# Decode attention over 65,536 keys on one core: every key chunk in the repeated code, alternating order of scores and values, second buffers

## The chip, the cores and the metric

The kernel runs on one core of one Trainium2 chip. The metric is the device time of one execution in microseconds. The profiler recorded one execution on the same core; "us" below is microseconds, and moments are counted from the first instruction of that execution.

## The reference

One query token, 32 query heads, 8 key/value heads, so that four query heads share one key/value head. Keys and values are bf16, 65,536 x 128 for each of the 8 heads: 134 MB of keys and 134 MB of values.

```python
B, Hq, Hkv, Sq, Sk, D = 1, 32, 8, 1, 65536, 128
k = jnp.repeat(k, rep, axis=1); v = jnp.repeat(v, rep, axis=1)
scores = jnp.einsum("bhqd,bhkd->bhqk", q, k) * D ** -0.5
p = _softmax(scores, axis=-1)
return jnp.einsum("bhqk,bhkd->bhqd", p, v)
```

## The kernel before

**Chunks.** Each head's keys are cut into four chunks of 16,384 keys, so there are 32 chunks (`NU`), and the key and value loads of chunk n are called K0 to K31 and V0 to V31 here. One load is 4,194,304 bytes: 128 partitions with 128 tiles of 128 values each. There are two buffers for keys (`kbuf`) and two for values (`vbuf`), so chunk n uses buffer n % 2.

**Loads.** SyncE issues every load on one DMA queue in the order K0, K1, V0, K2, V1, K3, V2, and so on. Before K(n) it waits for `kfree`, which ScalarE raises when TensorE has finished the transposes of chunk n-2. Before V(n) it waits for `vfree`, which VectorE raises when the value sum of chunk n-2 is done. A waiting load holds back all loads behind it in that order. K0 and K31 come in two pieces with semaphores of their own (`kpiece`), V31 in four (64, 32, 16 and 16 tiles, `vpiece`). The queries are loaded ahead of K0 on the same queue.

**TensorE.** A key tile must be transposed before it can be multiplied with the queries. The transposes go in 16 groups of eight tiles (`pe_transposes`). Each group lands in one of four PSUM buffers (`trb`) and is copied to `ktb` in SBUF (`evict`): three of four groups by VectorE, every fourth by ScalarE. The scores of a group (`pe_scores`) follow three groups later (`LAG`), so the transposes of group 15 are followed by the scores of group 12, and three score groups are still to come. `pe_values` multiplies the 128 value tiles of a chunk with its probabilities. `pe_pass(u)` runs the keys of chunk u+1 together with the values of chunk u: all transposes, with scores following; then the values of chunk u; then the last three score groups of chunk u+1. `passes` writes out the pass u = -1 (keys of chunk 0 alone), then a loop of 15 turns with two passes each, then the passes 30 and 31. Pass 31 has only the values of chunk 31.

**VectorE and the softmax.** For chunk u, `dve_pass(u)` first takes the value sum of chunk u-1 (L195), raises `vfree` (L196) and adds it to `acc`. Then it takes the finished scores of chunk u (`qkd`, L207) and reduces them to one maximum a partition (L212). It copies the first three groups of chunk u+1 and then waits for GpSimd's maximum over the partitions (L297, back through `cma`). It sets the new running maximum and hands the negated one to ScalarE (`ng`, L225 or L229). It copies the middle groups of chunk u+1, rescales the sums, and copies the last groups. ScalarE computes the probabilities into `pts` (L276), with four exponentials a chunk, and then tells TensorE that the values may start (`exd`).

**Start and end.** GpSimd builds the identity matrix (L292, L293) and VectorE casts it (L256). TensorE transposes the queries with it, and VectorE lays them out for the first head. Then TensorE waits for the first piece of K0. At the end VectorE adds the last value sum and divides by the sum of the probabilities (L202). TensorE transposes the result (L169), VectorE casts it (L263), and SyncE writes it out (L337).

Of the kernel before, what the change touches and what calls it, by code (L numbers as in the profile page):

```python
# [5 lines left out]
DT = mybir.dt  # L6
AF = mybir.ActivationFunctionType
ALU = mybir.AluOpType
# [7 lines left out]
NKG = 8  # L16
LAG = 3
HU = 4
K_PIECES = (64, 64)
V_PIECES = (64, 32, 16, 16)  # L20


# [10 lines left out]
def bass_standalone__gqa_softmax__decode_kernel(nc, q, k, v, out):  # L33
# [15 lines left out]
    def sem(name):  # L49
# [2 lines left out]
    kbuf = [sb(f"kbuf{i}", [P, T * D], DT.bfloat16) for i in range(2)]  # L52
    vbuf = [sb(f"vbuf{i}", [P, T * D], DT.bfloat16) for i in range(2)]
    ktb = sb("ktb", [P, NKG * TB * P], DT.bfloat16)
    pts = sb("pts", [P, T * R], DT.bfloat16)
    qsb = sb("qsb", [HR, D], DT.bfloat16)
    qT = sb("qT", [P, HR], DT.bfloat16)
    qtmp = sb("qtmp", [P, HR], DT.bfloat16)
# [18 lines left out]

    trb = [S(nc.psum_tensor(f"trb{i}", [P, TB * P], DT.bfloat16)) for i in range(NTB)]
    qkb = [S(nc.psum_tensor(f"qkb{i}", [P, T * R], DT.float32)) for i in range(2)]
    pvb = S(nc.psum_tensor("pvb", [P, 512], DT.float32))  # L80

    krdy = [sem(f"krdy{i}") for i in range(2)]
    vrdy = [sem(f"vrdy{i}") for i in range(2)]
    kpiece = [sem(f"kpiece{i}") for i in range(len(K_PIECES))]
    vpiece = [sem(f"vpiece{i}") for i in range(len(V_PIECES))]
    kfree = [sem(f"kfree{i}") for i in range(2)]
    vfree = [sem(f"vfree{i}") for i in range(2)]
# [3 lines left out]
    xd, xa, xg = sem("xd"), sem("xa"), sem("xg")  # L91
    q_sem, o_sem, s_x, t_if, t_id, t_qT, t_o, t_row = (
        sem(n) for n in ("q_sem", "o_sem", "s_x", "t_if", "t_id", "t_qT", "t_o", "t_row"))


    def has_k(u):
        return u + 1 < NU
# [13 lines left out]
    def pe_transposes(pe, n, j):  # L111
        b = n % 2
        kv = kbuf[b][:, :].rearrange("p (t d) -> p t d", d=D)
        pieced = n in (0, NU - 1)
        for i in range(TB):
            t = j * TB + i
            if not pieced and t == 0:
                take(pe, krdy[b], 16)
            if pieced and t in (0, K_PIECES[0]):
                take(pe, kpiece[t > 0], 16)  # L120
            ins = pe.transpose(trb[j % NTB][:, i * P:(i + 1) * P], kv[:, t, :], ident[:, :])  # L121
        ins.then_inc(tra if on_act(j) else trd, 1)

# [8 lines left out]
        if j == G - 1:  # L132
            ins.then_inc(qkd, 1)

    def pe_values(pe, u):
        vv = vbuf[u % 2][:, :].rearrange("p (t d) -> p t d", d=D)
        starts = [sum(V_PIECES[:i]) for i in range(len(V_PIECES))]
        for t in range(T):
            if u < NU - 1 and t == 0:
                take(pe, vrdy[u % 2], 16)  # L140
            if u == NU - 1 and t in starts:
                take(pe, vpiece[starts.index(t)], 16)
            if t == 0:
                take(pe, exd)
            ins = pe.matmul(pvb[:, 0:R], lhsT=vv[:, t, :], rhs=pts[:, t * R:(t + 1) * R],  # L145
                            start=t == 0, stop=t == T - 1)
        ins.then_inc(pvd, 1)

    def pe_pass(pe, u):
        pend = []  # L150
        if has_k(u):
            for j in range(G):
                pe_transposes(pe, u + 1, j)
                pend.append(j)
                if len(pend) > LAG:
                    pe_scores(pe, u + 1, pend.pop(0))
        if u >= 0:
            pe_values(pe, u)
        while pend:
            pe_scores(pe, u + 1, pend.pop(0))  # L160

    def tensor_engine(pe):
        pe.wait_ge(q_sem, 16)
        pe.wait_ge(t_id, 1)
        pe.transpose(trb[0][:, 0:HR], qsb[:, :], ident[0:HR, 0:HR]).then_inc(s_x, 1)  # L165
        pe.wait_ge(t_qT, 1)
        passes(pe, lambda u: pe_pass(pe, u), 0, 2, NU - 1)
        pe.wait_ge(t_o, 1)
        pe.transpose(qkb[0][0:HR, 0:P], oT[:, :], identf[:, :]).then_inc(s_x, 1)  # L169

# [16 lines left out]
    def next_queries(e, inc):  # L187
        e.tensor_copy(qcur[:, :], qT[:, 0:R]).then_inc(inc, 1)
        own(e, e.tensor_copy(qtmp[:, 0:HR - R], qT[:, R:HR]), xd)
        own(e, e.tensor_copy(qT[:, 0:HR - R], qtmp[:, 0:HR - R]), xd)  # L190

    def dve_pass(e, u):
        w = u - 1
        if w >= 0:
            take(e, pvd)  # L195
            e.sem_inc(vfree[w % 2], 1)  # L196
            if w % HU == 0:
                own(e, e.tensor_copy(acc[:, :], pvb[:, 0:R]), xd)  # L198
            else:
                own(e, e.tensor_tensor(acc[:, :], acc[:, :], pvb[:, 0:R], ALU.add), xd)  # L200
            if w % HU == HU - 1:
                e.tensor_tensor(oT[:, HR - R:HR], acc[:, :], recip[:, :], ALU.mult).then_inc(  # L202
                    t_o if w == NU - 1 else xd, 1)
                if w < NU - 1:
                    take(e, xd)
        if 0 <= u < NU:
            take(e, qkd)  # L207
            if u % HU == HU - 1 and has_k(u):
                next_queries(e, qrdy)
            elif has_k(u):  # L210
                e.sem_inc(qrdy, 1)
            e.tensor_reduce(cmax[:, :], qkb[u % 2][:, :].rearrange("p (t g) -> p g t", g=R),  # L212
                            AX.X, ALU.max).then_inc(cm, 1)
        if u >= NU:
            return
        part = [[j for j in range(a, b) if not on_act(j)] for a, b in ((0, 4), (4, 12), (12, G))]
        if has_k(u):
            for j in part[0]:
                evict(e, u + 1, j)
        if u >= 0:  # L220
            take(e, cma)
            mn, mo = m[u % 2], m[(u - 1) % 2]
            if u % HU == 0:
                e.tensor_copy(mn[:, :], cmaxa[:, :])  # L224
                e.tensor_scalar(negm[:, :], cmaxa[:, :], -scale, None, ALU.mult).then_inc(ng, 1)  # L225
            else:
                own(e, e.tensor_tensor(mn[:, :], mo[:, :], cmaxa[:, :], ALU.max), xd)
                e.tensor_tensor(dm[:, :], mo[:, :], mn[:, :], ALU.subtract)  # L228
                e.tensor_scalar(negm[:, :], mn[:, :], -scale, None, ALU.mult).then_inc(ng, 1)  # L229
        if has_k(u):  # L230
            for j in part[1]:
                evict(e, u + 1, j)
        if u >= 0:
            take(e, sx)
            if u % HU == 0:
                own(e, e.tensor_copy(lp[:, :], rsum[:, :]), xd)
            else:
                own(e, e.tensor_tensor(acc[:, :], acc[:, :], alpha[:, :], ALU.mult), xd)
                own(e, e.tensor_tensor(lp[:, :], lp[:, :], alpha[:, :], ALU.mult), xd)  # L239
                own(e, e.tensor_tensor(lp[:, :], lp[:, :], rsum[:, :], ALU.add), xd)  # L240
            if u % HU == HU - 1:
                e.sem_inc(lrd, 1)
        if has_k(u):
            for j in part[2]:
                evict(e, u + 1, j)
        if u % HU == HU - 1 and u >= 0:
            take(e, lra)
            own(e, e.reciprocal(recip[:, :], la[:, :]), xd)
            own(e, e.tensor_copy(otmp[:, 0:HR - R], oT[:, R:HR]), xd)
            own(e, e.tensor_copy(oT[:, 0:HR - R], otmp[:, 0:HR - R]), xd)  # L250

    def vector_engine(e):
        e.memset(oT[:, :], 0.0).then_inc(xd, 1)
        take(e, xd)
        e.wait_ge(t_if, 1)
        e.tensor_copy(ident[:, :], identf[:, :]).then_inc(t_id, 1)  # L256
        e.wait_ge(s_x, 1)
        own(e, e.tensor_copy(qT[:, :], trb[0][:, 0:HR]), xd)
        next_queries(e, t_qT)
        e.sem_inc(qrdy, 1)  # L260
        passes(e, lambda u: dve_pass(e, u), 1, HU, NU)
        e.wait_ge(s_x, 2)
        e.tensor_copy(orow[:, :], qkb[0][0:HR, 0:P]).then_inc(t_row, 1)  # L263


    def act_pass(e, u):
        if has_k(u):
            evict(e, u + 1, 3)
        if u >= 0:
            take(e, ng)  # L270
            if u % HU:
                e.activation(alpha[:, :], dm[:, :], AF.Exp, scale=scale)  # L272
            sv = qkb[u % 2][:, :].rearrange("p (t g) -> p g t", g=R)
            pv = pts[:, :].rearrange("p (t g) -> p g t", g=R)
            for g in range(R):
                ins = e.activation(pv[:, g, :], sv[:, g, :], AF.Exp, bias=negm[:, g:g + 1],  # L276
                                   scale=scale, accum_out=rsum[:, g:g + 1])
            own(e, ins, xa)
            e.sem_inc(exd, 1)
            e.sem_inc(sx, 1)  # L280
        if has_k(u):
            for j in (7, 11, 15):
                evict(e, u + 1, j)

    def scalar_engine(e):
        e.wait_ge(t_if, 1)
        e.activation(dscr[:, 0:1], identf[:, 0:1], AF.Exp, scale=1.0)
        passes(e, lambda u: act_pass(e, u), 1, HU, NU - 1)
# [14 lines left out]
    def sync_engine(e):  # L303
# [10 lines left out]
        def load_k(n):  # L314
            if n >= 2:
                e.wait_ge(kfree[n % 2], n // 2)
            if n in (0, NU - 1):
                pieces(kbuf[n % 2], src(kf, n), K_PIECES, kpiece)
            else:
                e.dma_start(kbuf[n % 2][:, :], src(kf, n)).then_inc(krdy[n % 2], 16)  # L320

        def load_v(n):
            if n >= 2:
                e.wait_ge(vfree[n % 2], n // 2)
            if n == NU - 1:
                pieces(vbuf[n % 2], src(vf, n), V_PIECES, vpiece)
            else:
                e.dma_start(vbuf[n % 2][:, :], src(vf, n)).then_inc(vrdy[n % 2], 16)

        e.dma_start(qsb[:, :], qf).then_inc(q_sem, 16)  # L330
        load_k(0)
        for u in range(NU):
            if has_k(u):
# [40 lines left out]
```

## Time and profile before

| What | Value |
| --- | --- |
| median of 3 runs | 638.78 us (637.18 to 639.63) |
| the profiled execution's own time | 639.29 us |
| its span, first to last instruction | 637.2 us |
| TensorE (matmul) busy | 505.6 us, 79% |
| VectorE, ScalarE, GpSimd busy | 310.4, 182.5 and 16.0 us |
| bytes moved | 268.69 MB, 422 GB/s over the span |
| TensorE's mean granted clock | 0.771 of full speed |

The shares of busy time are averages over the span. A row of a group names the line, the engine, what is written from what, how often, the busy time with the mean of one instruction, and after the bar the idle time of the engine just before these instructions with what ended it. "L30" is the wait inside the helper `take`, so the name behind it tells only that a semaphore was waited for. "issue" is time in which the engine waited for nothing that the profile shows.

### The profile page before, as it was taken

How to read it: one execution, taken by the hardware profiler on the slowest of the kernel's cores; microseconds unless marked ns; L12 is line 12 of the kernel's file. 1: busy time of each engine (PE TensorE's matmuls, PEld its weight loads, DVE VectorE, ACT ScalarE, POOL GpSimd, SP SyncE). 2: the span in 40 equal slices, each digit the busy share in tenths (PEclk: the TensorE clock that was granted, in tenths of full speed). 3: DMA queues.
4: the chain of work that ended last, by engine and by line, in shares of the span. 5: the costliest groups of instructions: out<-in, count | busy, mean ns of one | idle time of the engine just before them, and what ended most of it. 6: DMA issues, size and time to landing. Idle time of an engine off the chain costs nothing. (4 is left out here: it accounts for less than half of the span.)

```text
span 637.2 us, 27618 instructions
## 1 busy us (share of the span) xinstructions
PE 505.6 (79%) x12290; PEld 502.7 (79%) x12290; DVE 310.4 (49%) x676; ACT 182.5 (29%) x410; POOL 16.0 (3%) x46
## 2 busy tenths in 40 slices
PE   2847899889777798777897777887777977778885
PEld 2847899889777798777897777887777977778884
DVE  1533466555544465544555344654445554445561
ACT  0322133333221233221333222332213332223331
POOL 0000000000000000000000000000000000000000
PEclk9966788788767787767887678876778876688875
DMA  8999999999999999999999999999999999999994
GB/s 363 428 421 414 396 428 426 436 430 434 442 428 428 430 428 436 430 430 442 432 428 430 428 432 432 432 428 444 430 428 430 430 432 430 430 444 432 416 426 184
DMA packets 10049, 268.69 MB, mean 422 GB/s; under 512 B 1200, under 2 KB 1200, under 8 KB 1456
## 3 DMA queue, kind: packets, MB, share of 16 engines
q1 hardware_dynamic: 10032, 268.46, 98.4%
q8 instruction: 12, 0.20, 0.1%
q14 instruction: 5, 0.04, 0.0%
HBM read 268.44 MB, written 0.01 MB: 421 GB/s over the span
## 5 line engine op out<-in xcount | busy, mean ns | idle before, releaser
L121 PE MATMUL trb<-ident,kbuf 128*128 128x128 bf16 x4096 | 357.2, 246 | 95.8 <-PEq L30 93.0
L121 PEld LDWEIGHTS trb<-ident,kbuf 128*128 128x128 bf16 x4096 | 289.6, 111 | 99.1 <-issue 99.1
L181 DVE COPY ktb<-trb 128x1024 bf16<-128x1024 bf16 x384 | 255.4, 690 | 163.3 <-DVEq L30 162.1
L178 ACT ACTIVATE ktb<-trb 128x1024 bf16<-128x1024 bf16 x128 | 131.0, 1023 | 419.8 <-ACTq L30 419.8
L130 PE MATMUL qkb<-qcur,ktb 128*128 128x4 bf16 x4096 | 170.4, 165 | 12.4 <-PEq L30 7.3
L130 PEld LDWEIGHTS qkb<-qcur,ktb 128*128 128x128 bf16 x4096 | 155.0, 99 | 11.4 <-issue 11.3
L145 PE MATMUL pvb<-pts,vbuf 128*128 128x4 bf16 x4096 | 109.6, 165 | 8.8 <-PEq L30 6.8
L145 PEld LDWEIGHTS pvb<-pts,vbuf 128*128 128x128 bf16 x4096 | 107.4, 98 | 9.1 <-issue 9.1
L276 ACT ACTIVATE pts<-qkb,negm 128x128 bf16<-128x128 f32 x128 | 50.8, 551 | 9.7 <-ACTq L30 9.7
L200 DVE TENSOR_TENSOR acc<-acc,pvb 128x4 f32<-128x4 f32 x24 | 3.8, 159 | 74.9 <-DVEq L30 74.9
L276 ACT ACTIVATION_READ_ACCUMULATOR pts<-qkb,negm 128x1 f32 x128 | 36.0, 281 | 0.0
L212 DVE TENSOR_REDUCE cmax<-qkb 128x4 f32<-128x512 f32 x32 | 22.1, 692 | 13.9 <-DVEq L30 12.8
L297 POOL PARTITION_ALL_REDUCE cmaxa<-cmax x32 | 11.9, 371 | 522.0 <-POOLq L30 494.4
L198 DVE COPY acc<-pvb 128x4 f32<-128x4 f32 x8 | 1.3, 162 | 29.3 <-DVEq L30 29.3
L165 PE MATMUL trb<-ident,qsb 32*128 32x32 bf16 x1 | 0.2, 179 | 11.7 <-DVE ident L256 11.7
L165 PEld LDWEIGHTS trb<-ident,qsb 32*128 32x128 bf16 x1 | 0.1, 100 | 11.7 <-issue 11.7
L272 ACT ACTIVATE alpha<-dm 128x4 f32<-128x4 f32 x24 | 4.7, 197 | 8.0 <-ACTq L30 8.0
L224 DVE COPY m<-cmaxa 128x4 f32<-128x4 f32 x8 | 1.3, 161 | 9.6 <-DVEq L30 9.6
L239 DVE TENSOR_TENSOR lp<-lp,alpha 128x4 f32<-128x4 f32 x24 | 3.9, 163 | 3.5
L228 DVE TENSOR_TENSOR dm<-m 128x4 f32<-128x4 f32 x24 | 3.9, 162 | 3.5
L240 DVE TENSOR_TENSOR lp<-lp,rsum 128x4 f32<-128x4 f32 x24 | 3.9, 162 | 3.5
L300 POOL PARTITION_ALL_REDUCE la<-lp x8 | 3.4, 430 | 83.4 <-POOLq L30 83.4
(26 smaller groups left out, 27.1 us busy)
## 6 DMA issues: line engine op xcount, KB each, us to landing
vbuf<-in_v_dram SPq DMA_DIRECT2D x31, 4096.0 KB, 33.1
kbuf<-in_k_dram SPq DMA_DIRECT2D x30, 4096.0 KB, 26.8
kbuf<-in_k_dram SPq DMA_DIRECT2D x4, 2048.0 KB, 17.4
vbuf<-in_v_dram SPq DMA_DIRECT2D x1, 2048.0 KB, 20.5
vbuf<-in_v_dram SPq DMA_DIRECT2D x1, 1024.0 KB, 22.6
vbuf<-in_v_dram SPq DMA_DIRECT2D x2, 512.0 KB, 23.8
qsb<-in_q_dram SPq DMA_DIRECT2D x1, 8.0 KB, 1.6
out_dram<-orow SPq DMA_DIRECT2D x1, 8.0 KB, 1.4
```

The costliest lines, as they stand in the source:

```text
L121: ins = pe.transpose(trb[j % NTB][:, i * P:(i + 1) * P], kv[:, t, :], ident[:, :])
L130: ins = pe.matmul(qkb[n % 2][:, t * R:(t + 1) * R], lhsT=ktb[:, off:off + P], rhs=qcur[:, :], start=True, stop=True)
L145: ins = pe.matmul(pvb[:, 0:R], lhsT=vv[:, t, :], rhs=pts[:, t * R:(t + 1) * R], start=t == 0, stop=t == T - 1)
L178: e.activation(dst, trb[j % NTB][:, :], AF.Copy).then_inc(eva, 1)
L181: e.tensor_copy(dst, trb[j % NTB][:, :]).then_inc(evd, 1)
L212: e.tensor_reduce(cmax[:, :], qkb[u % 2][:, :].rearrange("p (t g) -> p g t", g=R), AX.X, ALU.max).then_inc(cm, 1)
L228: e.tensor_tensor(dm[:, :], mo[:, :], mn[:, :], ALU.subtract)
L239: own(e, e.tensor_tensor(lp[:, :], lp[:, :], alpha[:, :], ALU.mult), xd)
L240: own(e, e.tensor_tensor(lp[:, :], lp[:, :], rsum[:, :], ALU.add), xd)
L272: e.activation(alpha[:, :], dm[:, :], AF.Exp, scale=scale)
L276: ins = e.activation(pv[:, g, :], sv[:, g, :], AF.Exp, bias=negm[:, g:g + 1], scale=scale, accum_out=rsum[:, g:g + 1])
L297: e.partition_all_reduce(cmaxa[:, :], cmax[:, :], P, bass.bass_isa.ReduceOp.max).then_inc(cma, 1)
```

## The change

The change has four parts.

- **Repeated code.** TensorE's program becomes a loop of 16 turns with two chunks each, and the values of chunk 31 after it. So the keys of chunk 0 are now in the loop's first turn, and that turn also runs a value sum for a chunk "-1". Its inputs are `vbuf[1]` and `pts[1]`, which VectorE fills with zeros at the start, and its sum is dropped. VectorE raises the two semaphores that this sum waits for. Because it reads `vbuf[1]`, V1 now waits for `vfree[1]`, and every later load of an odd V waits for one more. K0 and K31 are loaded whole.
- **Order.** At even chunks n, the values of chunk n-1 come ahead of the last three score groups of chunk n, as before. At odd n they come after them.
- **Buffers.** `pts` and `pvb` are now two each. VectorE takes the value sum of chunk u-1 later in its pass: after the scores' reduction, the first three copies of chunk u+1, the wait for GpSimd's maximum and the new negated maximum.
- **Queries.** They are loaded on ScalarE's DMA queue.

```diff
+    pts = [sb(f"pts{i}", [P, T * R], DT.bfloat16) for i in range(2)]
+    pvb = [S(nc.psum_tensor(f"pvb{i}", [P, 512], DT.float32)) for i in range(2)]
...
     def pe_transposes(pe, n, j):
-        pieced = n in (0, NU - 1)
+        if j == 0:
+            take(pe, krdy[b], 16)
         for i in range(TB):
             t = j * TB + i
-            if not pieced and t == 0:
-                take(pe, krdy[b], 16)
-            if pieced and t in (0, K_PIECES[0]):
-                take(pe, kpiece[t > 0], 16)
...
-    def pe_pass(pe, u):
+    def pe_keys_values(pe, n):
         pend = []
-        if has_k(u):
-            for j in range(G):
-                pe_transposes(pe, u + 1, j)
-                pend.append(j)
-                if len(pend) > LAG:
-                    pe_scores(pe, u + 1, pend.pop(0))
-        if u >= 0:
-            pe_values(pe, u)
+        for j in range(G):
+            pe_transposes(pe, n, j)
+            pend.append(j)
+            if len(pend) > LAG:
+                pe_scores(pe, n, pend.pop(0))
+        if n % 2 == 0:
+            pe_values(pe, n - 1)
         while pend:
-            pe_scores(pe, u + 1, pend.pop(0))
+            pe_scores(pe, n, pend.pop(0))
+        if n % 2 == 1:
+            pe_values(pe, n - 1)
...
-        passes(pe, lambda u: pe_pass(pe, u), 0, 2, NU - 1)
+        with pe.Fori(0, NU // 2):
+            pe_keys_values(pe, 2)
+            pe_keys_values(pe, 1)
+        pe_values(pe, NU - 1, pieced=True)
...
+    def sum_values(e, w):
+        take(e, pvd)
+        e.sem_inc(vfree[w % 2], 1)
+        if w < 0:
+            return
+        pv = pvb[w % 2][:, 0:R]
...
     def dve_pass(e, u):
-        w = u - 1
-        if w >= 0:
-            take(e, pvd)
-            e.sem_inc(vfree[w % 2], 1)
...
                 e.tensor_scalar(negm[:, :], mn[:, :], -scale, None, ALU.mult).then_inc(ng, 1)
+        if u >= 0:
+            sum_values(e, u - 1)
+        if u >= NU:
+            return
         if has_k(u):
             for j in part[1]:
                 evict(e, u + 1, j)
...
     def vector_engine(e):
-        e.memset(oT[:, :], 0.0).then_inc(xd, 1)
-        take(e, xd)
+        e.memset(oT[:, :], 0.0)
+        e.memset(pts[1][:, :], 0.0)
+        own(e, e.memset(vbuf[1][:, :], 0.0), xd)
+        e.sem_inc(vrdy[1], 16)
+        e.sem_inc(exd, 1)
         e.wait_ge(t_if, 1)
         e.tensor_copy(ident[:, :], identf[:, :]).then_inc(t_id, 1)
...
     def scalar_engine(e):
+        e.dma_start(qsb[:, :], qf).then_inc(q_sem, 16)
         e.wait_ge(t_if, 1)
...
         def load_k(n):
             if n >= 2:
                 e.wait_ge(kfree[n % 2], n // 2)
-            if n in (0, NU - 1):
-                pieces(kbuf[n % 2], src(kf, n), K_PIECES, kpiece)
-            else:
-                e.dma_start(kbuf[n % 2][:, :], src(kf, n)).then_inc(krdy[n % 2], 16)
+            e.dma_start(kbuf[n % 2][:, :], src(kf, n)).then_inc(krdy[n % 2], 16)
 
         def load_v(n):
-            if n >= 2:
-                e.wait_ge(vfree[n % 2], n // 2)
+            if n >= 1:
+                e.wait_ge(vfree[n % 2], (n + 1) // 2)
...
-        e.dma_start(qsb[:, :], qf).then_inc(q_sem, 16)
         load_k(0)
```

## Prediction

> **What bounds the kernel now.** I read the page first, then the waits by engine, the timeline of both ends and the windows.
>
> ```profile
> span 637.2 us, 27618 instructions
> ...
> q1 hardware_dynamic: 10032, 268.46, 98.4%
> q8 instruction: 12, 0.20, 0.1%
> ```
>
> The load queue's packets fill 98.4% of the 16 engines' time, so the loads are the bound. The waits say the same. From 80 to 600 us TensorE waits only ahead of its transposes, for K to land; SyncE's own waits are long and harmless, since it queues loads far ahead.
>
> ```profile
> PE trb L121 <- PEq L30: 92.3, 25, 4.4
> ```
>
> ```profile
> SPq L320 <- ACTq L177: 454.7, 29, 24.4
> SPq L328 <- DVEq L196: 92.9, 29, 4.7
> ```
>
> TensorE has 92.3 / 25 = 3.7 us to spare in a chunk. From 80 to 620 us the windows give 431.5 GB/s, or 9.72 us for a load of 4.194 MB. Adding up the windows in steps of 1 us, I compared the bytes moved with a line of that slope. The stream is 1.10 MB behind it at the start (it begins at 2.55 us), 2.13 MB behind at 80 us, and no further behind afterwards. So 1.03 MB, or 2.4 us, is lost before 80 us, and the whole stream runs as if begun at 4.94 us. Two windows show where:
>
> ```profile
> 52.00:56.00 4.00, 3.37 (x114) 3.31 (x112) 0.28 (x2) 0.00 (x0) 0.00 (x0) 0.50 0.84 336
> ...
> 72.00:76.00 4.00, 2.63 (x101) 2.57 (x98) 0.00 (x0) 0.06 (x1) 0.00 (x0) 0.57 1.01 332
> ```
>
> (Last column: GB/s.) K3 was issued at 50.77 and K4 at 70.99 us, just too late. The timeline shows why:
>
> ```profile
> 0.80 0.09 DVE L253 MEMSET oT<- 128x32 f32 x1 [0.80 <-PEq L359]
> ...
> 10.99 0.28 POOL L293 TENSOR_SCALAR_AFFINE_SELECT identf<-identf 128x128 f32<-128x128 f32 x1 [10.07 <-issue]
> ...
> 25.53 0.33 SPq L320 DMA_DIRECT2D kbuf<-in_k_dram  x1
> 25.90 0.43 SPq L328 DMA_DIRECT2D vbuf<-in_v_dram  x1
> ...
> 27.33 0.69 DVE L212 TENSOR_REDUCE cmax<-qkb 128x4 f32<-128x512 f32 x1 [2.50 <-DVEq L30]
> ...
> 38.90 0.39 POOL L297 PARTITION_ALL_REDUCE cmaxa<-cmax  x1 [27.62 <-issue]
> ```
>
> GpSimd's first reduction starts 10.9 us after its input (28.02). VectorE, and so the transposes of chunk 1, wait for it. Also, TensorE pauses seven times before 80 us for "issue" (0.6, 2.3, 2.3, 0.6, 1.6, 0.8 and 1.4 us, mean 1.36), once in about 123 matmuls of code that it runs for the first time, and never between 80 and 600 us.
>
> The end is no longer the stream:
>
> ```profile
> 622.01 3.54 PE L145 MATMUL pvb<-pts,vbuf 128*128 128x4 bf16 x128 [2.66 <-PEq L30]
> 625.41 0.78 PE L130 MATMUL qkb<-qcur,ktb 128*128 128x4 bf16 x24
> 626.34 0.69 DVE L212 TENSOR_REDUCE cmax<-qkb 128x4 f32<-128x512 f32 x1 [0.39 <-DVEq L30]
> ...
> 630.37 3.56 PE L145 MATMUL pvb<-pts,vbuf 128*128 128x4 bf16 x128 [4.18 <-PEq L30]
> ```
>
> V30 lands at 622.0; its values, the last scores, and 4.2 us of softmax follow, and only then chunk 31's values, to 633.9.
>
> **The end, after the change.** Chunk 31 is odd, so its scores no longer wait for V30. Its softmax runs beside the values of chunk 30. K31 is whole now: K29 and K30 land at 571.65 and 591.07 (when their transposes begin), so K31 at 610.5 (before, its first half let TensorE start at 606.4). 11.4 us of transposes (as for chunk 30) reach 621.9; ScalarE's last copy (1.02) and the scores reach 623.4; 4.2 us of softmax, 627.6; 3.5 us of values, 631.1. The last piece of V31 (issued 607.4, landing 23.8 later: 631.2) leaves 16 matmuls, to 631.7. That is 2.2 us earlier than 633.9, and the 3.3 us behind stay. From below: a pause of 2.3 us in these values (code run once) leaves about 0.7 of the gain (the loop's exit before shows only 0.5); from above, 2.6. I take 2.2.
>
> **The start.** The queries leave SyncE's queue: K0 is issued at 0.72 instead of 1.17, and in one issue (0.43 instead of 0.88), so the stream begins at 2.1. On ScalarE the issue (0.39) lies in 9.3 us of idle time. Whole, K0 lands later: its first half landed 1.0 after the stream had passed those bytes, so all of it lands at 2.1 + 9.7 + 1.1 = 12.9; TensorE starts at 13.0 instead of 12.54.
>
> The two fills with zeros come ahead of the cast of the identity (11.3). The fills on the page cost 98 ns for 1 and 204 for 128 elements of four bytes, 0.835 ns each; the nearest row, VectorE's own, also has four-byte elements. `vbuf[1]` is 32,768 bytes a partition: 8,192 words, 6.9 us, done at 8.1; or 16,384 elements of bf16, 13.7 us, done at 15.1. Zeros are the same bytes either way; I take the words, hidden below 11.3, and keep the other as a rival. The Trainium skill (VectorE: DVE Perf Modes, "Zero memsets can be issued as uint32 (trn2)") says that a memset takes a cycle per element and that a zero fill can be issued in words. With its 0.96 GHz that makes 8.5 us in words, an estimate, also hidden, but 17.1 in bf16, which would begin the transposes at 19.9.
>
> From 13.0 on, by rows:
> - Transposes of chunk 0: 12.85 as before (12.54 to 25.39, with one pause), to 25.9. K2 is issued then (before 25.53), in time.
> - The empty value sum: 128 matmuls, 3.44. A pause falls in it (matmul 346 of the code): 1.36. Three score groups: 0.78. End 31.45 (before 27.09).
> - VectorE's maximum ends at 32.4; GpSimd starts 10.9 later at 43.3; the new maximum ends at 44.0. Only now, since the sum is taken behind it, does `vfree[1]` rise. V1 is issued at 44.2 instead of 25.9, and everything behind it on SyncE with it. Data follow an issue by 1.4 (1.17 to 2.55): 45.6. K2's data end at 2.1 + 4 x 9.72 = 41.0: the stream stands dry for 4.6.
> - K3: from VectorE's first copy after the maximum to its issue was 11.15 (39.62 to 50.77) with a pause of 2.26. Now one pause lies in the wait for GpSimd and one at the last transposes: 44.2 + 8.9 + 1.36 = 54.5, data 55.9, where V1 ends at 55.3: 0.6 dry.
> - V2 needs the values of chunk 0, now behind the scores: 54.4 + 1.4 (last copy, scores) + 3.44 + 1.36 (a pause) = 60.6. Then the transposes of chunk 2 until the third copy and the new maximum, 4.2 (571.65 to 575.24, plus 0.55): 64.8. Data at 66.3, K3 ends at 65.6: 0.7 dry.
> - K4: 60.6 + 11 = 71.6, data 73.0, needed at 76.0. From here TensorE gains on the stream; the repeated code has no pauses.
>
> Dry time 4.6 + 0.6 + 0.7 = 5.9, so an effective begin at 8.0. The same arithmetic on before gives 1.0 for K3, 0.8 for K4 and 4.35, where the bytes say 4.94: 0.3 more in each dry spell. Three spells: 8.9, or 4.0 later than 4.94. With the three pauses on this path at 0.6 or at 2.3 it is 1.3 or 6.8.
>
> **The rest.** The second buffers add no instruction. The later sum costs nothing once the stream has its lead: V(n+1) is issued some 4 us after K(n+1) has landed, with V(n) and K(n+2), up to 19 us of transfers, still ahead; VectorE's copies queued behind it find the sum finished. V31 is the tightest: issued at 614.8 instead of 606.1, data 616.2, V30's end 617.5 (1.3 to spare; without it the end moves by what is missing). A rule against the change: the Trainium skill (Runtime: NRT & Kernel Launch, "Instruction fetch mechanics") lets a taken branch to code outside the window force a fetch. This trace has 12 instruction packets on q8 for 15 turns, and no pause in them; were there one in each turn, it would fit into the 3.7 us.
>
> Sum, against the profiled execution's own 639.29 (2.1 outside its span): + 4.0 - 2.2 = 641.1. The median of the runs is 0.5 lower: 640.6. The main case runs from 1.3 - 2.6 to 6.8 - 0.7, or 637.5 to 644.9.
>
> **The rivals.**
> 1. GpSimd's 10.9 us do not start with its input, but end at 38.9 whatever happens. For: the same trace fits. Against: the 10.07 ahead of L293 is a like gap in place, and 27.6 is not. Then the maximum is at 39.6, V1's data at 41.3 (0.3 dry), K3 0.6, V2 0.7: begin at 5.5 with 0.3 for each spell, + 0.6 - 2.2: 637.2; with short pauses 634.5.
> 2. Slower: the fill in two-byte elements. It decides once it ends after 11.7 (13.0 less the 1.27 from L293's end to the first transpose). At 15.1 the transposes start at 16.4, 3.4 later, and so does the whole chain: 7.4 - 2.2, or 644.0.
> 3. The change doesn't do what it says: the empty sum delays as told, but a pause in the last values takes the end's gain: 4.0 - 0.7, or 642.1; this lies in the main case.
>
> **How the numbers follow.** A measurement of this kernel can tell about 0.5%, 3.2 us, from no change: 635.6 to 642.0 is "the same". Main case 0.70: 0.48 the same, 0.19 slower (pauses near their upper end), 0.03 faster. First rival 0.13: 0.06 faster, 0.07 the same. Second 0.14: slower 0.12, same 0.02. Left over 0.03: 0.01 each. Faster 0.10, same 0.58, slower 0.32. Range 636.0 to 645.5: the main case, most of the first rival, and the second.
>
> **What would show it.** V1 issued near 44 and K2's end followed by some 4.6 us without loads; no pause in chunk 2; the last values beginning near V31's landing and ending 0.5 behind it; VectorE's fill ending below 11. Wrong it would be if V1 were issued below 40, if the fill took 13 us or more, or if TensorE paused in every turn.

## The result, and the profile after

The changed kernel takes 643.87 us (median of 7 runs, 643.11 to 645.31). The kernel before took 639.23 beside it (7 runs, 637.18 to 641.85). The ratio is 1.0070 (95% interval 1.0046 to 1.0093): slower by 4.6 us, a little over the 0.5% that the prediction counts as a difference. The profiled execution took 643.11 us with a span of 641.1, against 639.29 and 637.2 before.

From the page of the changed kernel: the span, and the DMA queues (packets, MB, share of 16 engines' time).

```profile
span 641.1 us, 27880 instructions
...
q1 hardware_dynamic: 9696, 268.45, 97.8%
q8 instruction: 7, 0.11, 0.1%
...
q10 hardware_dynamic: 48, 0.01, 0.0%
```

The loads (q1) carry the same bytes in a longer span, so their share fell from 98.4 to 97.8%. The instruction packets fell from 12 to 7, and q10 is the queries on ScalarE's queue. The waits of TensorE and of SyncE (total us, times, longest):

```profile
PE trb L115 <- PEq L29: 77.6, 25, 4.4
```

```profile
SPq L334 <- DVEq L193: 331.6, 30, 19.2
SPq L326 <- ACTq L176: 247.3, 30, 23.6
```

From 80 to 600 us TensorE still waits mostly for K, 3.1 us a chunk; waits of at most 0.7 us ahead of scores add 9.2 us in all, which before did not have. SyncE now waits far longer for the value sums (331.6 us instead of 92.9), and less for the transposes. From 100 to 600 us the loads run at 432 GB/s, against 431 before, so that wait costs nothing in the middle of the kernel. The lost time lies at the start. The windows of the changed kernel (last column GB/s):

```profile
40.00:44.00 4.00, 0.00 (x0) 0.00 (x0) 0.00 (x0) 0.00 (x0) 0.00 (x0) 0.90 0.35 147
44.00:48.00 4.00, 1.81 (x30) 1.84 (x31) 2.56 (x6) 2.35 (x9) 0.39 (x1) 0.50 0.48 131
...
64.00:68.00 4.00, 4.00 (x75) 4.00 (x73) 1.38 (x2) 0.00 (x0) 0.00 (x0) 0.50 0.72 307
68.00:72.00 4.00, 4.00 (x76) 4.00 (x74) 2.94 (x8) 2.61 (x10) 0.00 (x0) 0.69 0.49 147
```

The stream stands nearly dry twice, from 41 and from 67 us on. The timeline has the chain behind both:

```profile
2.82 6.88 DVE L260 MEMSET vbuf<- 128x8192 uint32 x1 [1.66 <-issue]
11.01 0.28 POOL L302 TENSOR_SCALAR_AFFINE_SELECT identf<-identf 128x128 f32<-128x128 f32 x1 [10.08 <-issue]
...
31.74 0.67 PE L139 MATMUL pvb<-pts,vbuf 128*128 128x4 bf16 x19 [3.20 <-issue]
...
33.29 0.69 DVE L215 TENSOR_REDUCE cmax<-qkb 128x4 f32<-128x512 f32 x1 [8.90 <-DVEq L29]
...
44.42 0.39 POOL L306 PARTITION_ALL_REDUCE cmaxa<-cmax  x1 [33.13 <-issue]
...
45.18 0.33 SPq L334 DMA_DIRECT2D vbuf<-in_v_dram  x1
...
54.34 0.34 PE L115 MATMUL trb<-ident,kbuf 128*128 128x128 bf16 x3 [2.17 <-issue]
...
55.48 0.33 SPq L326 DMA_DIRECT2D kbuf<-in_k_dram  x1
...
63.66 1.60 PE L139 MATMUL pvb<-pts,vbuf 128*128 128x4 bf16 x55 [4.58 <-issue]
...
69.18 0.33 SPq L334 DMA_DIRECT2D vbuf<-in_v_dram  x1
```

The fill of `vbuf[1]` is done in words by 9.7 us and hidden. The empty value sum is held by a pause of 3.20 us, GpSimd answers 10.4 us after its input (33.98), V1 is issued at 45.18, K3 at 55.48, and V2, after one more pause of 4.58 us in the values of chunk 0, at 69.18. And the end:

```profile
629.69 3.52 PE L139 MATMUL pvb<-pts,vbuf 128*128 128x4 bf16 x128
629.83 0.69 DVE L215 TENSOR_REDUCE cmax<-qkb 128x4 f32<-128x512 f32 x1 [1.41 <-DVEq L29]
...
633.86 3.12 PE L139 MATMUL pvb<-pts,vbuf 128*128 128x4 bf16 x112 [0.66 <-PEq L29]
...
637.24 0.56 PE L139 MATMUL pvb<-pts,vbuf 128*128 128x4 bf16 x16 [0.25 <-PEq L29]
```

The last softmax now runs beside the values of chunk 30, and only 0.66 us of it is left as a wait. The last 16 matmuls wait for V31's last piece (0.25), so the end is the stream's again, by that quarter of a microsecond.

Two numbers sum this up, and all experiments below are read by them. The first is the **begin**: the moment at which a line of the steady rate, laid through the bytes moved from 200 to 560 us, starts from zero. The second is the **rest**, the span less the begin. Before: begin 5.1, rest 632.1. After: begin 11.7, rest 629.4. So the start costs 6.6 us and the end gives back 2.7, which leaves the 3.9 us between the two spans.

### The profile page after: what moved, and what is told of

The parts are those of the page before. It is cut to its first block, busy times and chain, and to the rows that moved or that the text cites. A ratio compares the mean times of both kernels' runs of the same rounds, so it can differ in the third digit from the quotient of the medians.

```text
span 641.1 us, 27880 instructions
## 1 busy us (share of the span) xinstructions
PE 514.7 (80%) x12418; PEld 510.0 (80%) x12418; DVE 316.2 (49%) x678; ACT 182.8 (29%) x410; POOL 16.1 (3%) x46
## 3 DMA queue, kind: packets, MB, share of 16 engines
q1 hardware_dynamic: 9696, 268.45, 97.8%
## 5 line engine op out<-in xcount | busy, mean ns | idle before, releaser
L139 PE MATMUL pvb<-pts,vbuf 128*128 128x4 bf16 x4224 | 114.1, 165 | 8.7 <-issue 7.8
L139 PEld LDWEIGHTS pvb<-pts,vbuf 128*128 128x128 bf16 x4224 | 111.9, 99 | 9.4 <-issue 8.9
L161 PE MATMUL trb<-ident,qsb 32*128 32x32 bf16 x1 | 0.2, 181 | 11.7 <-DVE ident L264 11.7
L161 PEld LDWEIGHTS trb<-ident,qsb 32*128 32x128 bf16 x1 | 0.1, 98 | 11.7 <-issue 11.7
L260 DVE MEMSET vbuf<- 128x8192 uint32 x1 | 6.9, 6885 | 1.7 <-issue 1.7
L187 DVE COPY qcur<-qT 128x4 bf16<-128x4 bf16 x8 | 1.4, 170 | 10.0 <-DVEq L29 9.9
```

Source lines behind the costliest of these rows:

```text
L139: ins = pe.matmul(pvb[u % 2][:, 0:R], lhsT=vv[:, t, :], rhs=pts[u % 2][:, t * R:(t + 1) * R], start=t == 0, stop=t == T - 1)
L260: own(e, e.memset(vbuf[1][:, :], 0.0), xd)
```

## The experiments

Theory: the begin is set by the single load that is issued latest for its place in the order, at its issue + 1.4 - 9.72 for each load ahead of it. What makes that load late is the chain of empty sum, GpSimd's first answer and TensorE's pauses. The rivals stand in the expectations. The edits of the first five (e1 to e5) are against the changed kernel, those of f1 to f3 against the kernel before; f4 and the last two name theirs. Ratios are to the kernel before, in runs on the same chip.

**e1, the empty sum is taken early.**

```diff
+        if u == 0:
+            sum_values(e, -1)
         if 0 <= u < NU:
             take(e, qkd)
...
-        if u >= 0:
+        if u > 0:
             sum_values(e, u - 1)
```

> The changed kernel, but the empty sum of chunk -1 is taken ahead of the first scores' reduction, so that V1 may be issued near 33 us instead of 45.2. Chain theory: the end of the stream is set by the last load that is issued too late, V2 (69.2 us), which waits for the values of chunk 0 and not for V1; V1 comes in time, the stream then stands dry some 6 us for K3 instead, and the time is that of the change within 1 us (643 to 645). Rival, each dry spell costs by itself: without V1's 4.6 us the time falls to about 639.

642.32 us, ratio 1.0045 (1.0026 to 1.0064). V1 is issued at 33.87, eleven us earlier, and the begin falls by only 1.2 us, to 10.5: K3 (54.72) and V2 (68.16) are hardly earlier.

```profile
33.87 0.33 SPq L336 DMA_DIRECT2D vbuf<-in_v_dram  x1
54.72 0.33 SPq L328 DMA_DIRECT2D kbuf<-in_k_dram  x1
68.16 0.33 SPq L336 DMA_DIRECT2D vbuf<-in_v_dram  x1
```

V1's delay, the longest dry spell of the changed kernel, cost next to nothing. The time lies a little below what was expected. One pause fell from 2.17 to 0.53 us, and that one now lay in the dry spell (see h1), which fits the 1.2 us.

**e2, every sum right behind the scores' reduction.**

```diff
                             AX.X, ALU.max).then_inc(cm, 1)
+        if 0 <= u != NU - 1:
+            sum_values(e, u - 1)
...
-        if u >= 0:
+        if u == NU - 1:
             sum_values(e, u - 1)
```

> The changed kernel, but every value sum (except that of chunk 30) is taken right behind the scores' reduction, ahead of the first three copies of the next chunk. Chain theory: V2 is issued as soon as the values of chunk 0 are done, near 65.3 instead of 69.2, in time for K3's end at 66.6; the stream gains 3 to 4 us, 640 in all. Rival, V2 is not what binds: within 1 us of the change.

640.94 us, ratio 1.0033 (1.0017 to 1.0049): some 3 us less than the change, still slower than before. The begin is 9.3. V2 comes at 64.65, as expected, and then the next link takes over: K4, issued at 76.64, is due at 76.64 + 1.4 - 7 x 9.72 = 10.0.

**e3, a first reduction on GpSimd at the start.**

```diff
                         base=0, pattern=[[-1, P]], channel_multiplier=1).then_inc(t_if, 1)
+        e.wait_ge(t_if, 1)
+        own(e, e.partition_all_reduce(wscr[:, :], identf[:, 0:R], P, bass.bass_isa.ReduceOp.max), xg)
```

(`wscr` is a new buffer)

> The changed kernel, with one more reduction over the partitions on GpSimd at the start, right behind the identity, whose result nothing reads. Chain theory: GpSimd's first maximum comes 0.4 us behind its input instead of 10.9, V1, K3 and V2 are issued some 10 us earlier (about 35, 46 and 59.5), the stream stands dry for less than 1 us, and the time is 634 to 635, less than both kernels. Rival, the empty sum and the pauses cost by themselves: still above 640.

635.94 us, ratio 0.9956 (0.9940 to 0.9972), less than both kernels, and 0.9 more than expected. GpSimd's timeline in this kernel:

```profile
22.29 0.39 POOL L306 PARTITION_ALL_REDUCE wscr<-identf  x1 [10.54 <-issue]
34.68 0.37 POOL L309 PARTITION_ALL_REDUCE cmaxa<-cmax  x1 [12.01 <-POOLq L29]
```

The 10.5 us are paid once, at the start, beside the landing of K0 and the first transposes. The begin falls by 6.2 us to 5.5. It is not 2.1, since V2 still comes at 63.02 (3.5 later than expected) because of pauses of 2.4 and 4.9 us, larger than I had allowed for.

**e4, values first at odd chunks too.**

```diff
-        if n % 2 == 0:
-            pe_values(pe, n - 1)
+        pe_values(pe, n - 1)
         while pend:
             pe_scores(pe, n, pend.pop(0))
-        if n % 2 == 1:
-            pe_values(pe, n - 1)
```

> The changed kernel, but odd chunks too have the values ahead of the last three score groups, as before. Theory: the order is worth the 3.0 us at the end (the stream runs 6.9 late, the time is 3.9 longer), so this kernel takes about 647. Rival, the end is bound by V31's landing and the order is worth nothing, or less than 1 us: 643 to 645.

643.12 us, ratio 1.0077 (1.0053 to 1.0102): no different from the change. By its time the rival is right; its trace says otherwise. The rest is 631.4, so undoing the order costs 2.0 us at the end, and the begin is 9.6, so it gains 2.1 at the start. Chunk 1 is odd too. With the values first, V2 is issued at 65.78 instead of 69.18, and the pause in those values is 0.90 instead of 4.58 us. So the gain at the start is not shown to be the order's alone: with a pause of 4.58 us V2 would have come at 69.46, no earlier than in the changed kernel. The instruction packet of the short pause came at 57.3 us, in the thin stretch between V1 and K3 (98 GB/s from 56 to 57 us); that of the long one came at 61.3, in the middle of K3's load:

```profile
60.20 0.94 PE L139 MATMUL pvb<-pts,vbuf 128*128 128x4 bf16 x29 [0.90 <-issue]
```

**f1, the first reduction on GpSimd in the kernel before** (the same two lines as in e3).

> The kernel before, with the additional reduction on GpSimd at the start. Chain theory: the 2.4 us that the stream loses before 80 us come from GpSimd's late first maximum, which holds the transposes of chunk 1 and so K3 and K4; K3 is issued near 41 and the time falls by 2 to 2.5 us, to about 637. Rival: TensorE's pauses alone make K3 and K4 late; within 0.7 us of before.

637.68 us, ratio 1.0005 (0.9987 to 1.0022): the rival by its time, though not by its cause. K3 is issued at 40.23, as expected, no load is late, and the begin is 2.9 instead of 5.1, so the stream did gain 2.1 us. But the profiled execution lost 1.2 at the other end (rest 633.3), where a pause of 0.95 us fell into the values of chunk 30; 637.2 to 636.2 is left in the spans, and less in the medians.

**f2, order and buffers in the kernel before.**

```diff
-        if u >= 0:
+        if u >= 0 and u % 2 == 1:
             pe_values(pe, u)
         while pend:
             pe_scores(pe, u + 1, pend.pop(0))
+        if u >= 0 and u % 2 == 0:
+            pe_values(pe, u)
```

(with the two buffers and the later sum of the change)

> The kernel before, with three things of the change: odd chunks' scores ahead of the values, two buffers for probabilities and value sums, and the value sum taken later on VectorE. The loop, the pieces of K0 and K31, the queries' queue and V1's wait stay as before, and there is no empty sum. Theory: the end's 3.0 us are gained, the later V2 costs at most 1 at the start: 636 to 637, about 2.5 less than before. Rival, the later sums make the start slow: 640 or more.

640.06 us, ratio 1.0027 (1.0006 to 1.0048): slower, where I expected 2.5 us less. The rest is 629.8 (2.3 gained) and the begin 8.3 (3.2 lost). V2 is issued at 65.24 instead of 55.18, behind the scores, the three copies and pauses of 3.4 and 4.0 us; V3 (85.11, due at 8.8) is then the latest. So the order with its buffers and the later sum gives less at the end than it costs at the start. In before those two pauses were 2.3 and 0.6 us, so a part of the cost is their length; no run separates the two.

**f3, f2 with the first reduction and the queries on ScalarE's queue.**

```diff
     def scalar_engine(e):
+        e.dma_start(qsb[:, :], qf).then_inc(q_sem, 16)
...
-        e.dma_start(qsb[:, :], qf).then_inc(q_sem, 16)
         load_k(0)
```

(with the edit of e3)

> The kernel before, with the order, the two buffers and the later sum, and besides the additional reduction on GpSimd and the queries on ScalarE's queue. Theory: the stream begins 0.45 earlier and loses nothing at the start (2.4 before), and the end's 3.0 us are gained: 633.5 to 634.5, less than both kernels. Rival: the loads can't run without dry spells because of TensorE's pauses; 636 or more.

635.94 us, ratio 0.9965 (0.9952 to 0.9978), less than both kernels, and 1.4 more than expected. The begin is 2.8, so no load is late. The rest is 631.0, since the code behind the loop brings two pauses into the last 15 us. TensorE's waits from 600 us on:

```profile
PE pvb L146 <- issue: 3.6, 2, 1.9
```

In the changed kernel and in e3 that row is absent, and their rest is 1.6 and 1.9 shorter: having every chunk in the repeated code is worth these pauses at the end.

**e5, the cures of e2 and e3 together.**

> The changed kernel with both cures: the additional reduction on GpSimd, and the value sums right behind the scores' reduction. Theory: what the change adds at the start is gone although the empty sum is still there, no load is late, and the time is 633 to 634.5, equal to the best of the others. Rival, the empty value sum costs by itself: 1 us or more above the kernel of before with order, reduction and queue.

636.87 us, ratio 0.9980 (0.9968 to 0.9992), no better than e3, so the expectation was missed by 2.4. The begin is 5.2. V2 comes in time at 59.72, but K4 does not (71.43, due at 4.8). f3, without the empty sum, begins at 2.8 although its sums are late. So the empty sum and the pause in it would cost some 2.4 us of begin that no cure here gave back. That is argued from a comparison and not shown: e5 and f3 also differ in the pieces of K0 and in the place of the sums. In the time, 0.9 of that is seen, a little less than the rival's 1 and not clear of the noise (the intervals overlap); f3 pays for its pauses at the end.

**h1, no loads in flight.** e3 with V1, and all loads behind it, held until the sum of chunk 0 is taken:

```diff
+        if u == 1:
+            e.sem_inc(hold, 1)
...
                 e.wait_ge(vfree[n % 2], (n + 1) // 2)
+            if n == 1:
+                e.wait_ge(hold, 1)
```

(`hold` is a new semaphore, and VectorE's loop begins one pass later, so that the first lines run once)

> The changed kernel with the additional reduction on GpSimd, and V1 (with every load behind it) held back until the value sum of chunk 0 is taken. So from about 41 us, when K2 has landed, no load is in flight while TensorE runs the rest of chunk 1 and the values of chunk 0 for the first time. Theory: TensorE's pauses in code run for the first time are fetches of instructions that wait behind load packets; then the pauses after 41 us, 2.4 and 4.9 us in the kernel without the hold, fall below 1 us each, and only those before 41 us stay as they were. Rival: the pauses belong to the code alone and stay at 2 to 5 us. The time itself is some 13 us longer, since the stream begins again only near 57 us.

650.5 us in one run, begin 18.2. The two pauses that lie after K2's landing, first in e3 and then with the hold (TensorE's timeline):

```profile
47.81 0.34 PE L116 MATMUL trb<-ident,kbuf 128*128 128x128 bf16 x3 [2.38 <-issue]
...
57.41 1.61 PE L140 MATMUL pvb<-pts,vbuf 128*128 128x4 bf16 x55 [4.86 <-issue]
```

```profile
43.71 0.69 PE L117 MATMUL trb<-ident,kbuf 128*128 128x128 bf16 x8
...
50.36 1.61 PE L141 MATMUL pvb<-pts,vbuf 128*128 128x4 bf16 x55 [1.68 <-issue]
```

The first is gone (the group of transposes is whole), the second is 1.68 us instead of 4.86. That is more than the 1 us of the expectation, but most of both pauses belonged to the loads in flight. It is one run, but the second pause, at the same place in the code, was 4.3 to 5.1 us in the changed kernel, e1, e2, e3 and e5. And f1 shows the reverse: TensorE runs the same code as before, its stream has no dry spell, and the two pauses in the values grew from 0.63 and 1.37 to 3.58 and 2.77 us. TensorE's waits from 10 to 80 us, before, in f1 and in the changed kernel:

```profile
PE pvb L145 <- issue: 2.0, 2, 1.4
```

```profile
PE pvb L146 <- issue: 6.3, 2, 3.6
```

```profile
PE pvb L139 <- issue: 7.8, 2, 4.6
```

In the changed kernel the first five packets of q8, 16 KB each, come 6.9, 7.3, 15.4 and 9.4 us apart, and the five pauses end 6.9, 7.2, 15.4 and 9.3 apart. Each pause ends 1.3 to 1.5 us behind the end of its packet, and the 1.68 us of h1 end 1.3 behind theirs. So a pause ends with an instruction packet; that the packet waits behind load packets is the reading that fits, not one that is shown. The values, which run through their code fastest, show the longest pauses.

**h2, loads in four pieces.** e3 with every load in four pieces of 32 tiles:

```diff
-            take(pe, krdy[b], 16)
+            take(pe, krdy[b], 64)
...
-            e.dma_start(kbuf[n % 2][:, :], src(kf, n)).then_inc(krdy[n % 2], 16)
+            pieces(kbuf[n % 2], src(kf, n), (32,) * 4, [krdy[n % 2]] * 4)
```

(and the same for V0 to V30)

> The changed kernel with the additional reduction on GpSimd, and every load issued in four pieces of 32 tiles, so that a packet is 8 KB a partition row instead of 32. Theory of waiting behind packets: a fetch waits for the packets that its engine has already taken, a fixed number of them; the packets are four times shorter, the pauses (0.6, 3.1, 1.8, 2.4 and 4.9 us) fall to less than half in sum, V2 is issued 4 us earlier or more, and the time falls to 632 to 634. Rival: what counts is the bytes queued ahead, or the load rate; the pauses stay within a fifth of 12.6 us in sum and the time within 1 us of 635.9, or more if smaller packets slow the stream.

649.13 us, ratio 1.0150 (1.0125 to 1.0176). The pauses fell from 12.6 to 8.7 us in sum, between the two expectations, V2 was issued 2.3 us earlier where 4 were expected, and the stream slowed:

```profile
80.00:620.00 540.00, 438.13 (x10627) 434.77 (x10624) 264.36 (x578) 154.81 (x347) 13.40 (x35) 0.76 1.01 422
```

A loss of 10 GB/s for the whole kernel costs far more than the pauses. How a fetch queues among the packets stays open.

**f4, f3 with chunk 31 in the loop.**

```diff
-        passes(pe, lambda u: pe_pass(pe, u), 0, 2, NU - 1)
+        pe_pass(pe, -1)
+        pe_pass(pe, 0)
+        with pe.Fori(0, NU // 2 - 1):
+            pe_pass(pe, 1)
+            pe_pass(pe, 2)
+        pe_pass(pe, NU - 1)
```

(K31 whole)

> The kernel before with order, buffers, additional reduction and queue, but with the keys of chunks 0 and 1 ahead of the loop and 15 turns that end with the keys of chunk 31 (K31 whole), so that only the values of chunk 31 are left as code run once at the end, and no empty sum is needed. Theory: the start stays free of late loads (begin near 2.9 us), the two pauses at the end (1.9 and 1.8 us) are gone or only one is left, and the time is 633.5 to 635. Rival: the pauses that now also fall into chunk 3 make K5 or V4 late and take it back: 636 or more.

635.31 us, ratio 0.9938 (0.9915 to 0.9961), the lowest median of all, though not clearly below e3 and f3. The rest is 629.7, without pauses, and the begin 3.7: V4 (99.90, due at 4.1) is now the late one, with K5 (89.29, due at 3.2) next, because the pauses reach into chunk 3.

**The begins against the theory.** Computed from the one latest load, and measured:

| Kernel | latest load, its issue | loads ahead | computed | measured | rest |
| --- | --- | --- | --- | --- | --- |
| before | K4, 70.99 | 7 | 4.4 | 5.1 | 632.1 |
| after | V2, 69.18 | 6 | 12.3 | 11.7 | 629.4 |
| e1 | V2, 68.16 | 6 | 11.2 | 10.5 | 629.8 |
| e2 | K4, 76.64 | 7 | 10.0 | 9.3 | 629.4 |
| e3 | V2, 63.02 | 6 | 6.1 | 5.5 | 629.1 |
| e4 | K3, 56.61 | 5 | 9.4 | 9.6 | 631.4 |
| e5 | K4, 71.43 | 7 | 4.8 | 5.2 | 630.9 |
| f1 | K0, 1.17 | 0 | 2.6 | 2.9 | 633.3 |
| f2 | V3, 85.11 | 8 | 8.8 | 8.3 | 629.8 |
| f3 | K0, 0.72 | 0 | 2.1 | 2.8 | 631.0 |
| f4 | V4, 99.90 | 10 | 4.1 | 3.7 | 629.7 |
| h1 | V1, 56.42 | 4 | 18.9 | 18.2 | 630.2 |

The one latest load gives each of these begins within 0.8 us. h2, whose stream runs at another rate, is not among them.

## Why the prediction was right or wrong

It gave 640.6 (636.0 to 645.5) and held "the same" for likeliest; the time is 643.9, in the range, but 4.6 us slower, which it had given a chance of 0.32. The case that came true is the main one, near its upper end. Of the 3.3 us that it lies above 640.6, 2.0 are in the profiled executions (643.1 against 641.1). The other 1.3 are scatter: the prediction took 0.5 off for the median, and the median came out 0.8 above the profiled execution.

- **The bound:** right. The loads bound both kernels, and the steady rate did not change.
- **The end:** right in kind, gain 2.7 instead of 2.2 us. The last values stopped for V31's last piece, as described.
- **The fill:** right. It ran in words, 6.88 us against the 6.9 worked out. It began 1.6 us later than reckoned and was done at 9.7 instead of 8.1, still below 11. The second rival fell with that. The Trainium skill (VectorE: DVE Perf Modes, "Zero memsets can be issued as uint32 (trn2)") agrees on the words; its cycle per element would make 8.5 us, an estimate, where the row has 6.9.
- **GpSimd:** right. Its first answer came 10.4 us after its input at its new place, and 10.5 in e3 at yet another. The first rival (ready at 38.9 in any case) is refuted. Its sum was wrong as well: 2.1 + 0.3 + 0.6 + 0.7 and 0.3 for each of three spells make a begin of 4.6 and not 5.5, so 636.3 and not 637.2.
- **The pauses:** the step that failed. "A pause falls in it: 1.36" and the two like it were set at the mean of the seven pauses of before, 4.1 us for three. (The second of the seven is 2.1 in its row, not 2.3; that changes the mean by 0.02.) They measured 3.20, 2.17 and 4.58, or 9.95, which is 5.9 more. Other links gave back 1.5 (GpSimd's answer 0.5 of it), so V2 was issued at 69.18 instead of 64.8, and the start cost 6.6 us instead of 4.0. I had taken seven pauses under different loads for one kind. Before's two pauses in values, 0.6 and 1.4, lay in its own two windows of thin load traffic (52 to 56 and 72 to 76 us); h1 and f1 show that loads in flight make most of the length. Two of the three pauses lie above the 2.3 that the range allowed for each. That the start still stayed inside 1.3 to 6.8 is in part luck, since the other links gave back 1.5.
- **The dry spells:** the sum 4.6 + 0.6 + 0.7 came out of the right arithmetic but told the wrong thing to mend. By e1 the 4.6 of V1 is worth almost nothing by itself, since the later loads would have been dry instead. The sum and the latest load (V2) give the same begin, 8.0, but only the latest load tells what to cure. The 0.3 for each spell was not needed either: with the measured issues the arithmetic gives 12.3 without it, where the bytes say 11.7.
- **The order at the start:** not priced by itself. The term for V2 has the values "now behind the scores", but the order was entered as a gain at the end alone. In e4 and f2 the order comes with a begin that is 2 to 3 us later, as much as the end gives; how much of that is the order and how much the longer pauses, no run separates.
- **The third rival** (a pause in the last values) did not happen: no pause from 600 us on.
- **The repeated code:** 7 instruction packets for 16 turns, and no pause in any turn but the first. The rule of the Trainium skill that spoke against it (Runtime: NRT & Kernel Launch, "Instruction fetch mechanics": a taken branch to code outside the window forces a fetch) cost nothing with this loop.

## What to carry to other kernels

When one queue of loads bounds a kernel, cost a change by two numbers: where the stream's line begins (its latest-issued load, by issue time less the transfers ahead of it) and what is left behind its last byte. Curing another late load moved next to nothing here (V1 in e1). A start-up cost of another engine, here GpSimd's some 10 us before its first reduction, belongs where nothing waits for it: two lines of code there took 7.9 us off the changed kernel, more than the whole change had lost. In the kernel before, the same two lines brought the stream 2.1 us forward and left the time the same.

## What the runs showed of the hardware

- GpSimd's first reduction over the partitions came 9.6 to 10.9 us after its input (before, the change, e1, e2, e4, f2). Where an additional one was put behind the identity matrix, GpSimd stood idle 9.5 to 11.3 us ahead of it. Later ones are free of that: the maxima take 0.37 us each, the sums 0.43.
- Code run for the first time on TensorE paused for 0.3 to 5.1 us about every 125 matmuls beside the load stream, and 0 and 1.68 us with no load in flight (h1, one run). Pauses whose instruction packet came in a dry or thin stretch were short (0.5 in e1, 0.9 in e4). Repeated code did not pause, in loops of 768 matmuls.
- Loads with 8 KB a partition row (h2) ran at 422 GB/s, those with 32 KB at 432.
